# The copy of chunk 0's x rows to the output moves behind the transposing DMAs of chunk 1

## The chip, the cores and the metric

The kernel runs on one core of one Trainium2 chip. The metric is the device time of one launch in microseconds (us). Engines are named as in the profile: PE (TensorE, matrix products), PEld (its weight loads), DVE (VectorE), ACT (ScalarE), POOL (GpSimd) and SP (SyncE, which here only issues DMAs; SPq is its queue).

## What is computed

One block of a network on 2048 rows of 640 numbers in bf16: a layer norm, and on its result an attention over 8 earlier positions in steps of 2 and a two-layer network; all three are summed.

```python
def _A_ref(x, wqkv, wo):            # S, D = 2048, 640;  H = 32 heads of 20
    ...                             # q, k, v = x @ wqkv, split
    W, dil = 8, 2
    idx = pos[:, None] - (jnp.arange(W) * dil)[None, :]
    ...
    logits = jnp.einsum("bhsd,bhswd->bhsw", q, kg) * scale
    attn = _softmax(jnp.where(mask[None, None, :, :], logits, -1e9), axis=-1)
    o = jnp.einsum("bhsw,bhswd->bhsd", attn, vg)
    return ... @ wo

def _B_ref(x, w1, b1, w2, b2):      # F = 1536
    return _gelu(x @ w1 + b1) @ w2 + b2

xn = _layernorm(x, axis=-1)
return x + _A_ref(xn, A_wqkv, A_wo) + _B_ref(xn, B_w1, B_b1, B_w2, B_b2)
```

## The kernel before

The 2048 rows are worked off in four chunks (n = 0 to 3) of 512 rows, each of four blocks (bl = 0 to 3) of 128 rows. All of x is loaded into `x_sb` with rows on partitions, one 128x640 slab for each block. For each chunk the stages are:

- Statistics of the layer norm, then the normalized block `xn` (`xn10` is chunk 1, block 0; for chunks 1 to 3 on ACT, line 266). `xn` tiles come from a pool of three buffers, so the fourth block of a chunk needs the first one's buffer back.
- The transposed block, written into `xnT` (128 features x 5 x 512 rows). For chunk 0 PE transposes; for chunks 1 to 3 it is a transposing DMA that SP issues, `do_td` (line 295). These pieces are called `tc10` to `tc13`; chunk 1's stand in the order tc13, tc10, tc11, tc12.
- The projections q, k, v (`pj`, line 339: chunk, which, column tile; `pj101` is the first of chunk 1) and their copies out of PSUM on ACT (`pc`). The first `pj` of a chunk waits for all four transposes.
- Logits: products q*k on DVE (`qk`, line 436), folded by DVE sums (`pa`, line 471) and summed per head on PE (`lg`, line 479); softmax (`cl` to `at`); the weights are spread over partitions by DMAs from SP (`xd`, line 554); products with v on DVE (`av`, line 563), summed by DVE and by adding DMAs from POOL (`aa`, line 573).
- The two-layer network: `f1` (line 595), gelu on ACT (`ge`), and `o`, which sums the second layer and the output projection in PSUM (lines 631 and 633).
- The result is added to the output rows in HBM by adding DMAs from POOL (`od`, line 644).

For those additions the output rows must hold something first. `do_xp` (line 304) copies x rows from `x_sb` to the output by a plain DMA from SP: `xp0` chunk 0 (640 KB), `xp1` chunk 1, `xp2` chunks 2 and 3 but for the last block (1120 KB). `do_xb` (line 308) then adds the bias b2 to these rows by an adding DMA from POOL: it needs the copy and the broadcast of b2, which SP loads behind `xp2` together with wo (`ldo`) and ahead of w2 (`ld2`).

The order of all work is written out by hand in `ORDER`, a list of pieces; every engine takes its instructions, and SP its DMAs, in the order of that list, and waits in order. Nothing is rescheduled. Names from the list stand in the text: `f10_9` is column tile 9 of the first layer for chunk 0, `su23` and `sq21` are row sums of chunk 2 on ACT.

Of the kernel before, what the change touches and what calls it, by code (L numbers as in the profile page):

```python
# [43 lines left out]
tp01 gb3 gb4 tc01a gd tc01b ho ge gc1 st03a st03 rs03 gc0 hj102 rc03 hc102 tb b1 hj101 hc101 st02a st02 rs02 hj100  # L44
hc100 xn03 tp03 tc03 pk hj202 rc02 xn02 tp02 tc02 gc4 hj201 hc201 hj111 st11a st10a hc111 st12a hj012 hc012 st11 hc202
st13a st13 hj112 hc112 st10 st12 rs1 qk010 rc1 qk000 qk011 hj110 f10_0 ge0_0 hj212 xn13 qk001 xn10 tc13 xn11 hc212
pa010 hj011 hj010 hc010 f10_11 f10_2 hc110 hc011 qk031 qk021 ge0_11 f10_10 xp0 qk020 pa000 su23 f10_6 xn12 ge0_10
qk030 pa020 su21 tc10 tc11 su22 hj200 hc200 f10_3 ge0_3 pa030 pa011 f10_9 tc12 su20 ng2 sq21 ge0_9 pa021 pj101 pc101
ge0_2 sq23 pj111 pj102 pj114 pc114 xp2 pc102 pj110 pc110 pj104 pa001 ge0_6 pa031 lg0 pc111 cl0 ldo xb3 xb2 pc104 mask
m0 mx0 ex0 pj112 pj103 pc103 pj113 pc113 ss0 ri0 pad11 pj100 pc100 pc112 qk121 qk120 hj211 sq20 hc211 qk101 ld2 pj124  # L50
qk100 sq22 pc124 f10_4 rs2 f11_6 pj121 rc2 ge0_4 pa120 qk110 f11_2 f10_1 ge0_1 pa121 qk111 xn21 pj123 pc123 ge1_6
# [745 lines left out]
```

## Time and profile before

| | us |
|---|---|
| median of 3 runs | 207.31 (206.66 to 207.37) |
| the profiled execution | 207.25 |
| its span in the trace | 205.3 |
| PE busy in the span | 200.1 |
| DVE busy | 181.6 |
| ACT busy | 127.1 |

The span is the time from the first to the last instruction in the trace; 1.95 us of the profiled execution lie around it. Busy time of an engine is that of its compute instructions; instructions that issue DMAs on SP are shown under SPq with the time that the issue took, and a landing is the time from the start of the issue until the data are there. A line of the timeline has start, duration, engine, source line, operation, output<-input, shape and count, and in brackets the idle time of the engine just before and what ended it. Merged lines (x10) have the duration of the whole group.

### The profile page before, as it was taken

The page shows a single profiled execution, that of the slowest core. Times are in us where ns is not written, and L with a number is a line of the kernel's source. Part 1 is how long each engine was busy: PE and PEld are TensorE (multiplying, and loading weights), DVE is VectorE, ACT ScalarE, POOL GpSimd, SP SyncE. Part 2 cuts the span into 40 slices and gives each one's busy share as a digit, 9 for nine tenths or more (in the row PEclk, how much of TensorE's full clock was granted, in tenths as well). Part 3 has the DMA queues.
Part 4 walks back from the last instruction along what each step waited for, and adds up shares of the span by engine and source line. Part 5 has one row for each costly group of instructions (what it writes and reads, how often), then busy time and mean ns, then how long its engine had stood idle before and what let it go on. Part 6 is the DMA issues. An engine that isn't in the chain of part 4 may idle for free.

```text
span 205.3 us, 3230 instructions
## 1 busy us (share of the span) xinstructions
PE 200.1 (97%) x1261; PEld 111.1 (54%) x1261; DVE 181.6 (88%) x226; ACT 127.1 (62%) x246; POOL 34.6 (17%) x49
## 2 busy tenths in 40 slices
PE   8899999999999999999999999999999999999994
PEld 3798655464454555554555555445544455555552
DVE  3489999389998999769999999899998999699992
ACT  6388998999966998856425735564535794111210
POOL 2000000440000242202260060003104223111120
PEclk9999999999999999999999999999999999999999
DMA  6999599899259299989999067005462997972253
GB/s 209 390 395 374 185 140 323 303 258 199 58 100 252 86 173 190 156 128 182 189 188 191 8 73 122 0 0 68 103 134 32 164 190 118 209 116 28 28 66 64
DMA packets 27335, 31.77 MB, mean 155 GB/s; under 512 B 9272, under 2 KB 22072, under 8 KB 27320
## 3 DMA queue, kind: packets, MB, share of 16 engines
q0 software_dynamic: 7408, 12.78, 39.0%
q1 hardware_dynamic: 19600, 18.58, 32.8%
q8 instruction: 10, 0.16, 0.3%
q10 hardware_dynamic: 312, 0.20, 0.3%
q14 instruction: 5, 0.04, 0.1%
HBM read 10.00 MB, written 7.54 MB: 85 GB/s over the span
## 4 chain that ended last, share of the span: by engine, by line
PE 90%; DMA 4%; ACT 3%; issue 1%; SPq 0%; DVE 0%
PE lo L631 29%; PE pps L339 24%; PE hps L595 22%; PE hi L633 7%; PE gps L383 5%; DMA wq_sb<-in_A_wqkv_dram 3%; DMA xnT<-xn 2%; ACT xn L266 2%; PE gps L352 1%; PE L L479 1%; ACT qT L398 1%; PE tp L283 0%; ACT trash L224 0%; ACT hT L611 0%; SPq L131 0%
## 5 line engine op out<-in xcount | busy, mean ns | idle before, releaser
L595 PE MATMUL hps<-xnT,w_sb 128*128 128x512 bf16 x240 | 55.6, 379 | 0.0
L436 DVE TENSOR_TENSOR half<-qT,kT 128x2560 bf16<-128x2560 bf16 x32 | 46.7, 1484 | 1.0 <-PE L L479 0.9
L631 PE MATMUL lo<-w_sb,hT 128*128 128x512 bf16 x144 | 41.3, 379 | 0.0
L595 PEld LDWEIGHTS <-w_sb 128*128 128x128 bf16 x240 | 23.1, 98 | 26.2
L471 DVE TENSOR_TENSOR half<-half 128x1024 bf16<-128x1024 bf16 (+1 forms) x44 | 36.5, 881 | 0.0
L638 ACT CAST osb<-lo 128x512 bf16<-128x512 f32 x15 | 8.8, 584 | 37.1 <-PE hi L633 18.3
L633 PE MATMUL hi<-w_sb,hT 128*128 128x128 bf16 x144 | 31.5, 219 | 0.0
L611 ACT ACTIVATE hT<-hps,b1T 128x512 bf16<-128x512 f32 x36 | 24.0, 692 | 6.5 <-PE hps L595 5.6
L563 DVE TENSOR_TENSOR half<-vT,x_sb 128x2560 bf16<-128x2560 bf16 x16 | 23.0, 1487 | 3.3 <-DMA x_sb<-e 3.2
L644 POOL DMA_DIRECT2D out_dram<-osb x15 | 13.7, 959 | 72.2 <-ACT osb L639 72.2
L573 POOL DMA_DIRECT2D half<-half x12 | 15.6, 1302 | 56.0 <-DVE half L563 56.0
L563 DVE TENSOR_TENSOR half<-vT,ax 128x2560 bf16<-128x2560 bf16 x16 | 23.0, 1482 | 1.2 <-PE L L479 1.2
L631 PEld LDWEIGHTS <-hT 128*128 128x128 bf16 x144 | 14.1, 98 | 17.2 <-issue 0.4
L631 PE MATMUL lo<-wo,oT 128*128 128x512 bf16 x80 | 23.1, 379 | 0.0
L339 PE MATMUL pps<-xnT,wq_sb 128*128 128x512 bf16 x75 | 18.5, 380 | 0.4 <-DMA xnT<-xn 0.4
L339 PE MATMUL pps<-xnT,wv_sb 128*128 128x512 bf16 x75 | 18.3, 379 | 0.0
L339 PE MATMUL pps<-xnT,wk_sb 128*128 128x512 bf16 x75 | 18.0, 379 | 0.0
L633 PE MATMUL hi<-wo,oT 128*128 128x128 bf16 x80 | 16.9, 219 | 0.0
L176 ACT ACT_TABLE_LOAD x12 | 15.4, 1283 | 0.9 <-PEq L781 0.7
L633 PEld LDWEIGHTS <-hT 128*128 128x128 bf16 x144 | 14.1, 98 | 1.9
L582 DVE TENSOR_TENSOR half<-half 128x1280 bf16<-128x1280 bf16 x16 | 13.1, 821 | 0.5 <-DMA half<-half 0.4
L403 ACT CAST vT<-pps 128x512 bf16<-128x512 f32 x15 | 8.8, 587 | 6.9 <-PE pps L339 6.9
(91 smaller groups left out, 262.3 us busy)
## 6 DMA issues: line engine op xcount, KB each, us to landing
half<-half POOLq DMA_DIRECT2D x12, 640.0 KB, 6.9
w_sb<-in_B_w_dram SPq DMA_DIRECT2D x4, 960.0 KB, 11.3
out_dram<-osb POOLq DMA_DIRECT2D x15, 160.0 KB, 3.5
ax<-e SPq DMA_DIRECT2D x8, 256.0 KB, 4.7
x_sb<-e SPq DMA_DIRECT2D x8, 256.0 KB, 4.9
out_dram<-b2bc POOLq DMA_DIRECT2D x3, 640.0 KB, 9.6
x_sb<-in_A_x_dram SPq DMA_DIRECT2D x1, 1280.0 KB, 12.9
out_dram<-x_sb SPq DMA_DIRECT2D x2, 640.0 KB, 4.7
```

Of the source, the lines that this page charges most:

```text
L176: nc.scalar.activation(warm[:], nc.const_aps.tensor(0.0, [P, 1], F32), func)
L339: nc.tensor.matmul(ps[:], lhsT=wqkv_p[which][:, ti, to, :], rhs=xnT[:, ti, :], start=(ti == 0), stop=(ti == KT - 1),)
L436: nc.vector.tensor_tensor(out=half[:, j, h], in0=q[:, :, at].unsqueeze(1).to_broadcast([P, W // 2, KT, P]), in1=window(k, h, at), op=ALU.mult,
L471: nc.vector.tensor_tensor(out=kept, in0=kept, in1=gone, op=ALU.add)
L563: nc.vector.tensor_tensor(out=half[:, j, h], in0=window(qkv_tile(n, 2), h, cs), in1=ax_view(n)[:, j, ws, :].unsqueeze(2).to_broadcast([P, ...
L573: nc.gpsimd.dma_start(a, b, accum_op=ALU.add, max_dma_last_dim=CUT)
L582: nc.vector.tensor_tensor(out=a, in0=a, in1=b, op=ALU.add)
L595: nc.tensor.matmul(ps[:], lhsT=w1_sb[:, ti, ft * P : (ft + 1) * P], rhs=tiles["xnT", n][:, ti, :], start=(ti == 0), stop=(ti == KT - 1),)
L611: nc.scalar.activation(hT, tiles["hps", n, ft][:], ACT.Gelu_apprx_tanh, bias=b1T[:, ft : ft + 1], scale=1.0)
L631: nc.tensor.matmul(lo[:], lhsT=lhs, rhs=rhs[:, 0:CH], start=first, stop=last)
L633: nc.tensor.matmul(hi[:, 0 : D - CH], lhsT=lhs, rhs=rhs[:, CH:D], start=first, stop=last)
L644: nc.gpsimd.dma_start(rows, tiles["osb", n, bl][:], accum_op=ALU.add)
```

## The change

`xp0` moves 20 pieces on in `ORDER`, from in front of `tc10`, `tc11` and `tc12` to just behind `tc12`. On SP the order "tc13, xp0, tc10, tc11, tc12, xp2, wo, b2, w2" becomes "tc13, tc10, tc11, tc12, xp0, xp2, wo, b2, w2". The instructions of the other four engines stand in the same order as before.

```diff
-pa010 hj011 hj010 hc010 f10_11 f10_2 hc110 hc011 qk031 qk021 ge0_11 f10_10 xp0 qk020 pa000 su23 f10_6 xn12 ge0_10
-qk030 pa020 su21 tc10 tc11 su22 hj200 hc200 f10_3 ge0_3 pa030 pa011 f10_9 tc12 su20 ng2 sq21 ge0_9 pa021 pj101 pc101
+pa010 hj011 hj010 hc010 f10_11 f10_2 hc110 hc011 qk031 qk021 ge0_11 f10_10 qk020 pa000 su23 f10_6 xn12 ge0_10 qk030
+pa020 su21 tc10 tc11 su22 hj200 hc200 f10_3 ge0_3 pa030 pa011 f10_9 tc12 xp0 su20 ng2 sq21 ge0_9 pa021 pj101 pc101
```

## The prediction

> **What bounds the kernel now.** I read the page first, for the engine that is never idle.
>
> ```profile
> PE 200.1 (97%) x1261; PEld 111.1 (54%) x1261; DVE 181.6 (88%) x226; ACT 127.1 (62%) x246; POOL 34.6 (17%) x49
> ...
> PEclk9999999999999999999999999999999999999999
> ```
>
> TensorE (PE) is busy for 97% of the span at full granted clock. Idle time elsewhere matters only where PE waits for it. So the second view is the list of PE's waits from 30.2 us to 202 us, and the third the busy time of that stretch. The list has one entry, and it is a wait for the transposes that the copy stands among:
>
> ```profile
> PE pps L339 <- DMA xnT<-xn: 0.4, 1, 0.4
> ```
> ```profile
> 30.30:202.40 172.10, 172.10 (x1034) 90.65 (x1034) 157.98 (x178) 103.44 (x197) 33.26 (x32) 1.00 0.70 134
> ```
>
> The second line reads: in 172.10 us PE was busy 172.10 us. From 30.30 us on there is nothing to win but less PE work, and the change removes none. What can be won lies at 30.28 us. The fourth view is the chain of waits around it, the fifth PE's timeline there, the sixth SyncE's queue (SPq), which issues both the copy (L304) and the transposes (L295).
>
> ```profile
> 25.73 0.81 ACT xn L266
> 26.54 0.03 ACT hT L611
> 26.56 3.58 DMA xnT<-xn
> 30.15 0.14 issue
> 30.28 2.76 PE pps L339 x12
> ```
> ```profile
> 27.53 2.32 PE L595 MATMUL hps<-xnT,w_sb 128*128 128x512 bf16 x10
> 30.28 1.25 PE L339 MATMUL pps<-xnT,wq_sb 128*128 128x512 bf16 x5 [0.43 <-DMA xnT<-xn]
> ```
> ```profile
> 21.12 1.32 SPq L295 DMA_TRANSPOSE xnT<-xn  x1
> 22.55 0.50 SPq L304 DMA_DIRECT2D out_dram<-x_sb  x1
> 23.11 5.79 SPq L295 DMA_TRANSPOSE xnT<-xn  x3
> 28.99 0.53 SPq L304 DMA_DIRECT2D out_dram<-x_sb  x1
> ```
>
> ACT finishes the last normalized block (xn12) at 26.54; SP issues its transpose, tc12, at 26.56; it lands 3.58 us later, at 30.15; 0.14 us after that PE starts pj101, the first product that reads chunk 1. How much PE loses: in the chain a group of five 128x512 products takes 1.08 us, so the ten that begin at 27.53 leave room for the next at 27.53 + 2.16 = 29.69. It starts at 30.28: **0.59 us lost**, of which the view counts 0.43 as idle (ends of matmuls are modelled).
>
> Then the transposes themselves, one window each. In the lines on landing, the first is tc10 (issued 23.11, just behind the copy), the second tc11 (24.88), the third tc12 (26.56), the fourth the same four transposes of chunk 2 at 53.65 to 57.64, with no copy near.
>
> ```profile
> DMA to landing us min/median/max: 5.8/5.8/5.8
> ```
> ```profile
> DMA to landing us min/median/max: 4.6/4.6/4.6
> ```
> ```profile
> DMA to landing us min/median/max: 3.6/3.6/3.6
> ```
> ```profile
> L295 SPq DMA_TRANSPOSE xnT<-xn x4: 1200/1218/1268, 53.6 to 57.6; - x4
> ...
> DMA to landing us min/median/max: 2.4/2.4/2.4
> ```
>
> Undisturbed: 1.2 us to issue, 2.4 us to land. Behind the copy: 5.8, 4.6, 3.6, a backlog that the last one still carries. tc12 also took 2.34 us to issue (26.56 to 28.90, where the second copy follows).
>
> **What the change removes there.** In program order tc10, tc11 and tc12 move ahead of the copy (xp0, 640 KB); PE, DVE, ACT and POOL keep their order. So SP goes 21.12 tc13 (1.32), then tc10 in the copy's place at 22.55 (its xn10 is ready: the three first xn end at 22.72, and xn11 is the last of them), issue 1.25 us, so tc11 at about 23.9, done at about 25.1. By the 2.4 us row they land at about 24.95 and 26.3. tc12 cannot be issued sooner than before: ACT ends xn12 at 26.54, and ACT has no gap before it. With nothing in front it lands at 26.56 + 2.4 = 28.96, where PE needs it by 29.69 - 0.14 = 29.55. There is 0.59 us to spare, so PE goes from its filler products into pj101 without a stop.
>
> Gain: bounds are 0 (tc12 still takes 3.58) and 0.59 us (2.4 to 2.99); more is excluded, since PE's earlier products would be the limit. I take 0.59: the undisturbed rows are four equal ones.
>
> **What the shift meets.** PE starts everything after 29.69 by 0.59 us earlier; is something else next? ACT waited 0.70 us for PE at 34.81, so it can follow. The logits (lg0, 36.86) need the last DVE sum, which ends at 35.97, and would now start at 36.27: 0.3 us are left. From there DVE's own next work waits for lg0 through ACT (2.66 us idle at 38.63), so DVE shifts as well, and at 65.78, where PE waits for DVE, both are earlier. After that all transfers that PE needs are issued behind DVE or ACT work of the same chain. Cost of this step 0, at worst the 0.59 lost again.
>
> **What the copy costs in its new place.** SP issues it at about 26.56 + 1.25 + 0.05 = 27.85, then the copy of chunks 2 and 3 (28.99 before) at about 28.4, then wo, b2's broadcast and two halves of w2, each some 0.55 us earlier than before. The same 640 KB now lies in front of these. It streams at about 400 GB/s, as the windows of 23.2 to 25 us show, so it takes 655 KB / 400 GB/s = 1.64 us. Against that, the stream may begin up to 28.99 - 27.85 = 1.14 us sooner. So everything behind comes between 0.5 and 1.64 us later; near 0.5, as the queue is no longer stuck. The covers:
> - w2: its halves are issued at 31.37 and 32.3 and take 11.3 us; PE's first use is at 54.07. Some 10 us cover 1.64. wo is first used later still. Cost 0; without cover, up to 1.64.
> - b2: POOL waits for it until 38.91, then issues the three sums onto the output (L308, landing in 7.2 to 12.1 us, the last at 52.7) and the memset of vT's padding at 41.36, which DVE first reads at 66.38. POOL's next work is at 69.57. Cost 0.
> - the output rows: POOL adds onto chunk 0's rows only after the copy has landed, now about 31.5; the first such sum of chunk 0 is the third, issued at 40.61. x_sb's first rows are overwritten from 86.59. Cost 0.
> - the waits of the moved instructions are on loads that landed long before (x, wk, wv).
>
> A rule of the Trainium skill bears on the price: "DMA: Bandwidth & Descriptors", section "Queues, rings and completion order", has each DMA engine take one row's descriptors in ring order. By that rule of the Trainium skill alone the copy delays what stands behind it by its own stream, and tc12, issued after the copy had landed, by nothing: the sum would be 207.25, which is the first rival below. The trace shows the order (256-byte packets follow the copy's) but goes beyond the rule: tc10 is 3.4 us late where the stream explains 1.64.
>
> Sum: 207.25 us (profiled execution; span 205.3 and 1.95 around it) - 0.59 + 0 = 206.66. That execution is 0.06 from the median of 207.31, so I say **206.7**.
>
> **Rivals.**
> *No gain.* What stalls the transposes may not be the copy. The DMA view of 25 to 26.4 us and the one of 26.4 to 28.6 us have these rows:
>
> ```profile
> q8 instruction: 1, 0.02, 8.1%
> q14 instruction: 2, 0.02, 5.5%
> ```
> ```profile
> DMA packets 351, 0.09 MB, mean 40 GB/s; under 512 B 351, under 2 KB 351, under 8 KB 351
> ```
>
> The copy has landed at 22.55 + 3.5 = 26.05, but then the transposes crawl at 40 GB/s for 2.2 us, just after instruction blocks were fetched through the same DMA engines: 8.1% of 16 x 1.4 us, or 1.8 us, on one engine. If such a fetch still holds tc12, it lands at 30.15 as before: 207.25. Against it: in the new order tc10 and tc11 are through before 26.3, and tc12's own packets start about 1.2 us after its issue (the windows at 53 us), at 27.8, when the fetch that began by 26.4 should be over. The same section of the Trainium skill has an engine switch between queue rows at packet boundaries; by it a fetch costs the transposes a share of one engine, no standstill, which the 40 GB/s of the trace speaks against.
>
> *Slower.* The delayed b2 sums run into the transposes of chunk 2. The last of them landed at 52.7; the first of chunk 2 is issued at 53.65 (53.06 when shifted) and its packets start some 1.15 us later, at 54.2. With 1.64 us of delay the last sum lands at 54.3; from there on they share the DMA engines. Transposes beside such sums landed in 7.0 us at 94.66, and beside others in 4.1 at 87.25, against 2.4: 1.7 to 4.6 us late. pj200, at 61.37, has its last transpose at 57.64 + 2.4 = 60.04, a slack of 1.3. So PE would lose 0.4 to 3.3 us there, net of the gain -0.2 to +2.7: 207.1 to 210.0. From 5.3 us of landing on it is a slowdown that counts (2.4 + 1.3 + 0.59 + 1.04). For: the fourth xn of chunk 2 starts at 56.11, just when the first transpose has landed (53.65 + 2.4) and its buffer is free, so each delay is passed on; and three loads are stacked behind the copy, so 1.64 need not be all. Against: with 0.5 us of delay the sums end at 53.2 and touch nothing.
>
> *A larger gain*, were ACT's work before 26.54 also slowed by the copy's reads: ACT's 128x640 sums take 0.74 to 0.76 us there and 0.73 at 58.07, so under 0.1 us; 206.1 at best by some part that I don't see.
>
> **How the numbers follow.** The forecast gets 0.62 (its own range 206.3 to 207.0), no gain 0.15, slower 0.18, a larger gain 0.05. 0.5%, about what a measurement of this kernel can tell from no change, is 1.04 us; the forecast moves 0.59, and the three runs spread over 0.7 (206.66 to 207.37), so I give 0.13 of its 0.62 to being read as faster. Faster 0.13 + 0.05 = 0.18; same 0.49 + 0.15 = 0.64; slower 0.18. The range goes from the larger gain, 206.1, into the lower half of the slower rival, 208.0.
>
> **What would show it.** Right: SPq with four L295 in a row from 21.1 and L304 near 27.9; tc12 landing in about 2.4 us; no PE wait on xnT near 29.7; PE busy throughout after it; the first use of b2 by POOL near 39.4. No gain: tc12 again at 3.6. Wrong: a PE wait of over 0.5 us on xnT at 61, or any new PE wait behind 30 us.

## The result and the profile after

The changed kernel takes 206.05 us (median of 18 runs, 205.67 to 207.06) against 206.93 us for the kernel before (18 runs): the ratio is **0.9967, 95% interval 0.9957 to 0.9978**, that is 0.68 us less, between 0.46 and 0.89. (The two medians lie 0.88 us apart, the two means 0.71; the ratio and its interval are the figures to go by.) The same kernel in a second series gave 0.9972 (0.9953 to 0.9990). The profiled execution took 206.31 us, its span 204.5 us.

The page's first line, and PE's waits from 29 us to 202 us:

```profile
PE 200.3 (98%) x1261; PEld 111.4 (54%) x1261; DVE 181.6 (89%) x226; ACT 127.2 (62%) x246; POOL 34.6 (17%) x49
```
```profile
PE L L479 <- DVE half L471: 0.2, 1, 0.2
```

PE's work is the same; its wait on xnT is gone. One short wait of another kind has come, at 127.7 us (below). SyncE's queue and PE's timeline:

```profile
20.43 6.68 SPq L295 DMA_TRANSPOSE xnT<-xn  x4
27.21 1.08 SPq L304 DMA_DIRECT2D out_dram<-x_sb  x2
```
```profile
26.85 2.32 PE L595 MATMUL hps<-xnT,w_sb 128*128 128x512 bf16 x10
29.01 1.24 PE L339 MATMUL pps<-xnT,wq_sb 128*128 128x512 bf16 x5
```

The four transposes stand in a row, the copy behind them. The ten filler products, the last that read chunk 0 before chunk 1's turn, begin at 26.85, and 26.85 + 2.16 = 29.01 is to the hundredth where pj101 starts. Landing of tc10 and tc11 together, then of tc12:

```profile
DMA to landing us min/median/max: 2.4/3.5/4.5
```
```profile
DMA to landing us min/median/max: 2.4/2.4/2.4
```

tc12 takes 2.4 us instead of 3.6. tc11 does not: 4.5 us, with no copy ahead of it. The section "What holds up tc11" and several of the runs ahead of it are about the reason.

How the 0.75 us between the two profiled spans (205.30 and 204.55) came about, by PE's starts: its first product on chunk 0, the first that needs the weights wq, at 6.09 instead of 6.77 us (-0.68, long before the changed place); pj101 another 0.59 earlier; and 0.57 lost again at 128 us. That makes 0.70; the other 0.05 were not followed. Only the middle one is in the edited stretch.

### The profile page after: what moved, and what is told of

Its sections match the earlier page's. It is cut to its first block, busy times and chain, and to the rows that moved or that the text cites. A ratio compares the mean times of both kernels' runs of the same rounds, so it can differ in the third digit from the quotient of the medians.

```text
span 204.5 us, 3231 instructions
## 1 busy us (share of the span) xinstructions
PE 200.3 (98%) x1261; PEld 111.4 (54%) x1261; DVE 181.6 (89%) x226; ACT 127.2 (62%) x246; POOL 34.6 (17%) x49
## 4 chain that ended last, share of the span: by engine, by line
PE 75%; DVE 15%; DMA 5%; ACT 2%; issue 1%; SPq 1%; DVEq 0%; ACTq 0%
PE lo L631 23%; PE hps L595 20%; PE pps L339 17%; PE gps L383 7%; PE hi L633 6%; DVE half L436 5%; DVE half L471 5%; DMA x_sb<-e 3%; DVE half L563 3%; PE gps L352 1%; DVE half L582 1%; DMA x_sb<-in_A_x_dram 1%; PE L L479 1%; DVE oT L586 1%; PE tp L283 1%
```

## The experiments

All are compared with the kernel before on the same chip. Two numbers are followed: how long tc12 took to land, and PE's loss before pj101, which is pj101's start less the filler's start and 2.16 us. Both are from one profiled execution of each kernel, the ratio from all its runs.

| kernel | tc12 landing, us | PE loss, us | ratio to before (95%) |
|---|---|---|---|
| before | 3.58 | 0.59 | 1 |
| changed | 2.36 | 0 | 0.9967 (0.9957 to 0.9978) |
| changed, second series | 2.38 | 0 | 0.9972 (0.9953 to 0.9990) |
| copy left out | 2.39 | 0 | 0.9978 (0.9969 to 0.9988) |
| copy ahead of tc13 | 2.37 | 0 | 0.9994 (0.9941 to 1.0047) |
| half in the old place | 3.00 | 0 | 1.0000 (0.9979 to 1.0022) |
| between tc11 and tc12 | 3.38 | 0.40 | 0.9996 (0.9977 to 1.0015) |
| double in the old place | 4.31 | 2.11 | 1.0090 (1.0070 to 1.0110) |
| on ACT's queue | 3.88 | 0.89 | 1.0040 (1.0011 to 1.0069) |

A loss depends on two things, how long tc12 takes and how much time it has. With PE and ACT as far apart as in the kernel before, tc12 is issued 0.97 us ahead of the filler and may take 2.99 us before PE waits. In the runs with the double copy and with moved blocks of instructions that distance is smaller, so their loss is not the price of the landing alone.

A second kind of traffic comes up in most of these runs, the blocks of instructions of the first rival. In the packet records of the kernel before there are three near 26 us: two of 8 KB (q14 in the DMA views), from 26.08 to 26.39 and from 26.12 to 27.05 us, and one of 16 KB (q8) from 26.00 to 27.82. The block of 16 KB holds PE's instructions, it seems: with 60 more of these at the start it began at 20.66 us (the fourth run below).

### Between tc11 and tc12

```diff
-... xp0 qk020 ... su21 tc10 tc11 su22
+... qk020 ... su21 tc10 tc11 xp0 su22
```

> The copy stands between tc11 and tc12, so only the last transpose is behind it. Theory Q (a transpose waits for whatever stands ahead of it in SP's queue): tc10 and tc11 land in 2.4 us, the copy is issued some 25.2 us into the kernel and streams for 1.64 us, so tc12, issued near 26.5, starts only when it is through: landing 3.6 to 5.8 us after issue instead of 2.4, PE's wait before pj101 as long as before the change or longer (0.6 to 2.8 us): 206.9 to 209. Theory F (the copy is harmless, the instruction fetch near 26 us holds up the transposes that are in flight then): tc12's packets come after the fetch as in the changed kernel, landing under 3 us, no PE wait: 206.1.

The chain of waits and PE's timeline:

```profile
25.99 3.38 DMA xnT<-xn
29.37 0.14 issue
```
```profile
26.95 2.32 PE L595 MATMUL hps<-xnT,w_sb 128*128 128x512 bf16 x9
29.51 1.25 PE L339 MATMUL pps<-xnT,wq_sb 128*128 128x512 bf16 x5 [0.23 <-DMA xnT<-xn]
```

(x9 where ten are meant: one record is missing from the trace, here and in two rows below.) tc12 is 1.0 us late and PE loses 29.51 - 26.95 - 2.16 = 0.40 us; at 0.9996 no gain is left that stands clear of the noise. The copy ahead of the last transpose is enough: it landed at 28.77, tc12 0.60 us behind it, while the last block of instructions had ended at 26.35, 3.0 us before. So here theory Q has the cause right and theory F has not. Q's sizes were too high: 3.38 and 0.40 us lie below the lower ends that it gave, 3.6 and 0.6.

### Ahead of all four

```diff
-... xn13 qk001 xn10 tc13 ...
+... xn13 qk001 xn10 xp0 tc13 ...
```

(and xp0 goes from its old place)

> The copy stands ahead of all four transposes, where SP is idle: it can be issued near 14 us, when chunk 0's rows have landed, and its bytes move behind the load of chunks 2 and 3 (landed near 21.9 us). Theory Q: tc13 may land up to 1.6 us later, but the backlog is gone before tc12 is issued; tc12 lands in 2.4 us, no PE wait: 206.1, as the changed kernel. What counts then is when the copy's bytes move, not that it stands ahead. Theory F: the same. If the copy's writes to HBM slow the transposes at any distance, a wait remains: 206.9.

SP issues the copy at 12.18 us. tc12 lands in 2.37 us and PE loses nothing, as expected; so to stand ahead costs PE nothing when the bytes are gone in time. The median, 205.99 us, fits, but the five runs scatter (to 208.53) and the interval takes in no change: on the time this run decides nothing. In the profiled execution, which took 207.67 us, PE's first product came at 7.91 us, 1.8 us later than in the changed kernel's, ahead of anything the edit touches.

### Twice the bytes

```diff
-            piece(f"xp{n}", do_xp, n, (1, 2, 4)[n])
+            piece(f"xp{n}", do_xp, n, (2, 2, 4)[n])
```

In its old place xp0 now writes chunks 0 and 1 together, and xp1 goes.

> In the old place, one copy of chunks 0 and 1 (1280 KB, twice the bytes; the separate copy of chunk 1 near 63 us falls away). Theory Q: another 1.64 us of stream ahead of tc10 to tc12; tc12 lands about 5.2 us after issue, PE's wait before pj101 grows from 0.6 to about 2.2 us: 208.5. Theory F: the transposes go when the fetch is over and the wait stays at 0.6: 206.9.

```profile
27.26 2.32 PE L595 MATMUL hps<-xnT,w_sb 128*128 128x512 bf16 x9
31.53 1.25 PE L339 MATMUL pps<-xnT,wq_sb 128*128 128x512 bf16 x5 [1.95 <-ACT trash L231]
```

The loss is 31.53 - 27.26 - 2.16 = 2.11 us; the view names ACT, but tc12, issued at 27.08, had landed only at 31.39. 208.39 us, where theory Q said 208.5. tc12 itself took 4.31 us and not the 5.2 that Q gave; the rest of the loss is that SP, still busy with the issue of tc11, could not issue tc12 when xn12 was ready at 26.27 but 0.81 us later. From xn12's end to the landing it is 5.12 us. So the price grows with the bytes. It is not shown that the copy's own stream is all of it: the blocks of instructions, too, began only when this copy was through (27.78 to 28.05, the copy landed at 27.86; 25.1 to 25.3 in the run without a copy), and tc10 landed 1.2 us after the last of them had ended. Theory F's 0.6 us supposed blocks near 26 us; with the blocks so late this run does not decide between the two.

### The instruction fetch: PE's block moved away

```diff
-        do_warm(WARM, CH)
+        do_warm(4 * WARM, CH // 4)
```

> The kernel before, with PE's ten warm-up products of 512 columns at the start cut into forty of 128 columns: the same time of warming, but 60 more PE instructions, so each later block of PE's instructions is fetched some 6 us earlier (near 19.5 us instead of 26). The copy stays ahead of tc10 to tc12. Theory Q: tc12 still lands in 3.6 us, PE still waits: 206.9. Theory F: with no fetch among them the transposes flow as soon as the copy has streamed (about 25.0 us), tc10, tc11 and tc12 land at about 26, 27 and 29, no PE wait: 206.3.

The DMA view of 25.3 to 26.6 us has no q8 row any more, the two blocks of q14 are still there:

```profile
q1 hardware_dynamic: 914, 0.29, 99.6%
q14 instruction: 2, 0.02, 5.7%
```
```profile
27.16 2.32 PE L595 MATMUL hps<-xnT,w_sb 128*128 128x512 bf16 x9
29.84 1.25 PE L339 MATMUL pps<-xnT,wq_sb 128*128 128x512 bf16 x5 [0.36 <-DMA xnT<-xn]
```

tc10 lands in 5.1 us, tc11 in 3.9, tc12 in 2.9 (before: 5.8, 4.6, 3.6), PE still loses 29.84 - 27.16 - 2.16 = 0.52 us. Neither theory as written: the wait stays, yet each landing is 0.6 to 0.7 us shorter. The wait stays for another reason: in this run tc12 was issued only 0.37 us ahead of the filler (26.79 and 27.16) and had 2.39 us. With the 2.99 us of the kernel before, a landing of 2.91 would have been in time. The run itself is slower than before (1.0024, 1.0006 to 1.0041), so the cut warm-up costs something of its own.

### All three blocks moved

```diff
+    for _ in range(8):
+        nc.scalar.activation(warm[:], nc.const_aps.tensor(0.0, [P, 1], F32), ACT.Sqrt)
+    ...
+    for _ in range(14):
+        nc.vector.memset(spare[:], 0.0)
```

(with the edit of the run above; `spare` is a new 128x1 tile)

> The kernel before, copy in its old place, with instructions added at the start so that all three blocks of instructions which were fetched near 26 us are fetched earlier: forty narrow PE warm-up products for ten wide ones (PE's block near 20 us), 8 small ACT and 14 small DVE instructions (theirs before 25 us). Theory QF (the copy alone does no harm to PE; it pushes tc10 and tc11 back to where the fetches hold up whatever transposes are in flight): with no fetch left there tc10 to tc12 run through after the copy, tc12 lands in about 2.4 to 2.6 us, PE's wait before pj101 is gone or under 0.2 us. Theory Q (the copy alone delays them): tc12 lands in 2.9 us or more and PE waits 0.4 us or more. The added instructions may themselves cost some tenths of a us at the start, so the verdict lies in the wait, not in the total: 206.3 to 207.5.

```profile
L300 SPq DMA_TRANSPOSE xnT<-xn x1: 1199/1199/1199, 27.6 to 27.6; - x1
...
DMA to landing us min/median/max: 2.6/2.6/2.6
```

One of the three blocks, of 8 KB, was still fetched among the transposes, at 27.2. tc10, tc11 and tc12 land in 4.5, 3.2 and 2.6 us with the full copy as far ahead of them as in the kernel before: the last is the value that theory QF gave, and no more than an undisturbed transpose takes in this run (2.57 to 2.64 for the four of chunk 2); the first is still some 2 us late. PE's wait did not go (30.38 - 27.34 - 2.16 = 0.88 us), and that tells nothing: the added ACT work made xn12 late against PE, tc12 was issued at 27.64 and had to land within 1.7 us, which no transpose of any run does. The expectation had picked the wrong number to judge by. The time, 208.23 us, lies above the 206.3 to 207.5 that were expected; besides the 0.88 us PE waits another 0.5 for chunk 3's transposes at 104.6 us in the profile, and the rest was not followed.

### Another queue

```diff
-        nc.sync.dma_start(dst, x_sb[:, cs, :])
+        (nc.scalar if n == 0 else nc.sync).dma_start(dst, x_sb[:, cs, :])
```

and `xp0` right behind `xn12` in `ORDER`.

> The copy is issued by ACT, right behind xn12, at the moment when SP issues tc12: another queue, the same 16 DMA engines. If a transpose waits only for what stands ahead of it in its own queue, tc12 shares the engines by turns: its 0.6 us of packets take up to twice as long, landing at most 3.0 us, no PE wait, 206.1. If engines are shared to the transposes' disadvantage, tc12 lands 1.0 to 1.6 us late as behind the copy in the run with the copy between tc11 and tc12, and PE waits 0.4 to 1.0 us: 206.5 to 207. ACT itself loses some 0.5 us of its queue for the issue, which its waits for PE near 34 us can take in part.

```profile
23.43 0.42 ACTq L304 DMA_DIRECT2D out_dram<-x_sb  x1
...
25.23 0.94 ACT L266 ACTIVATE xn<-x_sb,nmr,rstd 128x640 bf16<-128x640 bf16 x1
```

The copy was not issued behind xn12: ACT's sequencer had sent it off 1.8 us before xn12 began, together with tc11 (23.47). So it ran beside tc11, on another queue, and the run is not the one that was planned. tc11 took 6.07 us and tc12 3.88, PE lost 0.89 us, 1.0040. The time has more in it than that loss: in the profile PE waits another 0.93 us at 104.48, for chunk 3's transposes, and whether that belongs to the edit is open. Being in another queue does not spare the transposes. The rule weighed in the prediction (the Trainium skill, "DMA: Bandwidth & Descriptors", section "Queues, rings and completion order", ring order within a row) cannot be the reason here: tc10 had landed at 24.56, and nothing else stood ahead of tc11 in its ring. Here, too, the blocks of instructions came late, at 27.18 to 27.30, as the copy landed (27.10), so copy and blocks are not told apart.

### Half the bytes

```diff
+    def do_xh(b0, b1):
+        nc.sync.dma_start(out_sd.rearrange("(b p) d -> p b d", p=P)[:, b0:b1, :], x_sb[:, b0:b1, :])
...
+            piece("xp0", do_xh, 0, 2)
+            piece("xh0", do_xh, 2, 4)
```

`xp0` stands in the old place, `xh0` behind tc12.

> Half the dose: the copy of the first two blocks of chunk 0 (320 KB) stays in the old place, that of the other two goes behind tc12. If the delay of tc12 is the copy's stream carried on in the queue (1.2 us late for 640 KB, 1.9 for 1280 KB by the runs), half of it leaves tc12 0.3 to 0.6 us late: landing 2.7 to 3.0 us. If the copy matters only because it pushes tc10 into the fetches near 26 us and the backlog of that is handed on, then tc10, 0.8 us earlier than behind the full copy, is mostly through before the fetches, only tc11 is held up, as in the changed kernel, and tc12 lands in 2.4 to 2.6 us. PE needs it within 2.99 us of its issue, so PE has no wait in either case: 206.1.

```profile
22.64 5.13 SPq L295 DMA_TRANSPOSE xnT<-xn  x3
27.82 0.57 SPq L307 DMA_DIRECT2D out_dram<-x_sb  x1
```
```profile
DMA to landing us min/median/max: 3.0/3.0/3.0
```

tc10 took 4.9 us, so the half copy was enough to push it into the fetches, though its own bytes had landed at 24.49, and tc12 is 0.6 us late: half of the full copy's 1.2. PE lost nothing in the profile, but 3.0 us is the very limit, and the time (1.0000, 0.9979 to 1.0022) shows no gain clear of the noise; 206.1 had been expected and 206.66 was measured. Not explained further: a profile shows one execution, and this one lies on the edge.

### No copy at all

```diff
-... f10_11 f10_10 xp0 qk020 ...
+... f10_11 f10_10 qk020 ...
```

> The copy of chunk 0's x rows is left out altogether (the output rows of chunk 0 then lack x). If the copy costs nothing in its new place, this takes as long as the changed kernel, 206.1, with tc12 in 2.4 us and no wait of PE on xnT. If the moved copy still costs PE something, this is faster than the changed kernel by that; b2's sums come some 1.6 us sooner than there (near 37 us instead of 38.5).

```profile
27.11 2.32 PE L595 MATMUL hps<-xnT,w_sb 128*128 128x512 bf16 x10
29.27 1.24 PE L339 MATMUL pps<-xnT,wq_sb 128*128 128x512 bf16 x5
```

206.21 us and 0.9978 (0.9969 to 0.9988), tc12 in 2.39 us, no wait. Its interval and the changed kernel's overlap: the copy in its new place costs nothing that these runs can tell, as the prediction's covers had it. tc11 still takes 4.0 us there.

### What holds up tc11

With no copy anywhere, tc10 and tc12 land in 2.4 us and tc11 in 4.0; in the changed kernel's two profiles tc11 takes 4.5 and 4.3. The changed kernel's DMA view of 25 to 26.4 us:

```profile
GB/s 80 31 15 1 242 22 483 22 15 22 15 22 8 0 0 0 0 0 0 0 0 0 0 0 0 0 0 0 0 0 0 0 0 0 0 0 0 0 0 0
...
q8 instruction: 1, 0.02, 6.4%
q1 hardware_dynamic: 67, 0.01, 4.1%
q14 instruction: 1, 0.01, 3.2%
```

40 columns of 0.035 us: from 25.45 on next to nothing moves but the blocks of instructions. The one of q8 takes 6.4% of 16 x 1.4 us, 1.43 us, and as it is a single packet, on one engine; by the packet records it ends at 26.64. The last packets of SP's queue ahead of tc12's, two of 4 bytes, come at 26.62 and 26.63, and tc11 has landed at 27.70 (issued 23.16). So a transpose that is in flight then is held until the fetch is over, with or without the copy. In the new order this falls on tc11, which has time: PE needs the data at 28.87. In the old order it fell on tc10, with tc11 and tc12 queued behind it.

The packet records of the other runs say the same. In all twelve profiles the first transpose of chunk 1 that met the blocks landed 0.8 to 1.3 us after the last block had ended, wherever that end lay (26.34 to 29.04 us). In the four with no copy near and all three blocks (the changed kernel twice, the copy left out, the copy ahead of tc13) tc11 landed 1.06 to 1.10 us after it.

That these fetches are the cause is shown in part by moving them. With the copy in the old place, moving one of three blocks took 0.67 us off tc12's landing and moving two 0.97 of 1.22 us. In the new order, with the block of 16 KB moved away (the last run below), tc11's row reads

```profile
DMA to landing us min/median/max: 3.3/3.3/3.3
```

where it had been 4.0 to 4.5. The run without any of the blocks among the transposes was not reached.

### The second profile, and the wait at 128 us

> The changed kernel once more, unaltered, for a second profile. Its first profile won 0.6 us at 30 us and lost 0.57 us at 128 us, where PE waited for DVE. If that loss belongs to the change, it is here again; if it comes and goes with the moment at which an instruction fetch meets the spreading DMAs near 94 us, it may be absent. Either way no wait of PE on xnT near 29 us, the last transpose of chunk 1 in 2.4 us, and 206.1 (0.997 of before).

DVE's wait for the last of the spreading DMAs of chunk 1, in the first profile of the changed kernel and in the second:

```profile
96.45 5.70 DVE L563 TENSOR_TENSOR half<-vT,x_sb 128x2560 bf16<-128x2560 bf16 x4 [1.29 <-DMA x_sb<-e]
```
```profile
95.89 5.69 DVE L563 TENSOR_TENSOR half<-vT,x_sb 128x2560 bf16<-128x2560 bf16 x4 [0.60 <-DMA x_sb<-e]
```

From there DVE has no idle time to make it up until it feeds PE's sums at 128 us. With the longer wait PE is late there (0.57 us), with the shorter it has no wait of its own from 28 us to 203 us. Nor does PE wait at 128 us in any profile of another kernel here. In the views of 93 to 97 us the fetched block of q8 took 2.8% of 16 x 4 us in the first and 2.1% in the second, 1.8 and 1.3 us. So the loss comes and goes and is no constant price of the change.

### The changed kernel with PE's block moved

The same edit of `do_warm` on the changed kernel.

> The changed kernel with PE's warm-up cut into forty narrow products, so that all later blocks of PE's instructions are fetched 60 instructions earlier (near 87 us instead of 93.8 us). If that fetch held up the last spreading DMA of chunk 1 and cost PE the 0.57 us at 128 us, DVE's second wait on x_sb (1.3 us at 96.4) is back to some 0.2 us and PE has no wait at 128: 206.0 or a little less. If not, both stay: 206.1. The cut of the warm-up alone cost the kernel before some 0.2%, so 206.5 would be no surprise; the waits decide.

```profile
96.74 5.69 DVE L563 TENSOR_TENSOR half<-vT,x_sb 128x2560 bf16<-128x2560 bf16 x4 [0.50 <-DMA x_sb<-e]
```

DVE's second wait on x_sb, 1.29 and 0.60 us in the two profiles of the changed kernel, is 0.50 here, and PE does not wait at 128 us. (A wait of 1.3 us is still there, but it is DVE's first one on x_sb, at 90.5, which is 1.1 to 1.5 us long in every kernel here.) That is the way that was expected, though not back to 0.2; and as the second profile of the changed kernel had no wait at 128 us either, with its block in the old place, it proves little. PE's block was now fetched near 90.5 us, where the first transpose of chunk 3 was in flight: 5.6 us to land instead of 4.1, so the fetch moved from one victim to another. The link between the fetch at 94 us and the 0.57 us is likely, not shown. The time was a miss: 1.0051 (1.0037 to 1.0066), slower than the changed kernel by some 1.6 us, where 206.0 to 206.5 were expected. The cut warm-up cost the kernel before 0.24%, 0.5 us; PE's small waits in this profile (0.15 us at pj101, 0.2 at 36.8 us, twice 0.2 behind 191 us) make up another part, and the rest was not followed.

## Why the prediction was right

The sign, the size of the change and the path by which PE gains it were right; 0.59 us was forecast, 0.68 (0.46 to 0.89) and in the second series 0.58 (0.21 to 0.97) were measured. As a time the forecast was off: the 206.7 us lie 0.65 above the measured 206.05, which is 0.05 below the 206.1 at which the range began. About half of that is the starting point: the sum counted from one profiled execution of 207.25, in which PE began late, and 18 runs put the kernel before at 206.93.

- *PE's loss of 0.59 us at pj101, and nothing else to win*: measured 0.59 between the two profiles, 0 left.
- *tc12 undisturbed in 2.4 us*: 2.36 and 2.38. tc10 likewise (2.4). The step that failed is tc11: 2.4 forecast, 4.5 and 4.3 measured. The fetch was seen in the first rival but not carried into the new order, where by the sum's own times (tc11 in flight from 23.9 to 26.3) it had to meet tc11. That it cost nothing is luck as far as the prediction goes: tc11 landed 1.17 us before PE needed it, a slack that the sum had not worked out.
- *The copy in its new place at 0*: issued at 27.21, which with the 0.68 us of earlier start is 27.89 against the 27.85 of the sum; leaving it out wins nothing more.
- *b2's sums, the slower rival*: they were issued from 38.51 and the last landed at 52.4; all four transposes of chunk 2 took 2.4 us. The delay of the sums, 0.3 us against the common start, was below the lower bound of 0.5. The price of 1.7 to 4.6 us that this rival used was not tested, and its upper end is not that of the sums alone: the transpose issued at 94.66 met a block of instructions too (94.93 to 95.86 in the packet records).
- *The shift carried to the end*: right in one profile, lost for 0.57 us in the other, where PE has a short new wait behind 30 us, which the prediction itself had named as a sign of being wrong. The sum had checked the waits up to 66 us and taken the rest as one chain; the spreading DMAs near 94 us are where it breaks.
- *The first rival, no gain*: its cause, the fetch, is a real part of the delay, but the gain does not need it gone. Neither "the copy" nor "the fetch" alone describes the loss: the copy pushes tc10 to where the blocks are fetched, the fetch holds it, and tc11 and tc12 land one after another behind it. A copy directly ahead of tc12 is enough by itself (the run between tc11 and tc12); how the 1.2 us of the old place divide between the two is open.

## What to carry to other kernels

When the bound engine waits once, for a short chain of DMAs, look for bulk transfers that nobody waits for and that run at the same moment, and move them behind, not to another queue: what counts is when the bytes move, not in which queue they stand (tc12 in 2.37 us with the copy early and ahead of it, in 3.88 with the copy beside tc11 in ACT's queue). Measure the gain as the late start of the waiting product against the steady beat before it (0.59 us here, the idle time shown was 0.43), and expect no more than that. Kernels with spans that vary by several tenths of a us at the start need the comparison inside the stage (tc12's landing, PE's loss), since one profile's total can hide or fake such a gain.

## What the runs showed of the hardware that was not expected

- A transposing DMA that is in flight while blocks of instructions are fetched lands late even with no copy near: 4.0 to 4.5 us instead of 2.4, with the DMA engines otherwise nearly idle, and 1.06 to 1.10 us after the end of the 16 KB block. With that block moved away and two of 8 KB left it took 3.3 us.
- In two runs the blocks themselves began only as a copy landed: at 27.78 to 28.05 us with the double copy (landed at 27.86) and at 27.18 to 27.30 with the copy on ACT's queue (27.10), against 25.1 to 25.3 in the run without a copy.
- A DMA issued on ACT's queue left 1.8 us ahead of an ACT instruction that stands before it in program order and that it doesn't depend on (issued at 23.43, xn12 began at 25.23). So the order of the list holds for what ACT computes, not between that and a DMA on its queue.
- PE's first product of chunk 0, the first that needs wq, began anywhere from 6.03 to 7.91 us in nine profiled executions of kernels that differ only in where the copy stands, how large it is, on which queue, and whether there is one; it starts later than that in all of them. The latest start, 7.91, belongs to an execution of 207.67 us, 1.68 above the median of its kernel.
